# Four edits in the first stage of a fused attention and SwiGLU kernel: a narrower row spread, squares summed in eights, x^T of block 0 copied inside the chip, and one added wait on GpSimd

## The chip, the cores and the metric

The kernel runs on one core of one Trainium2 chip. A core has a matrix engine (TensorE, PE in the profile, with its weight loads listed apart as PEld), a vector engine (VectorE, DVE), an activation engine (ScalarE, ACT), a general engine (GpSimd, POOL) and a queue processor that mostly starts transfers (SyncE, SP). Each engine works through its own instruction list in order and waits on semaphores. SBUF is the core's working memory of 128 partitions; PSUM holds TensorE's results. Transfers (DMAs) are carried by 16 DMA engines, which all queues share.

The metric is the time of one execution on the device in microseconds (us), lower is better.

## The reference

One input x of 2048 tokens by 512 features goes through a layer norm; the result feeds both a 32-head softmax attention (head size 16) and a SwiGLU feed-forward of width 1792, and the two are combined by a gate:

```python
xn = _layernorm(x, axis=-1)
s = _A_ref(xn, A_wqkv, A_wo)                             # attention, 32 heads of 16, then wo
g = _silu(_B_ref(xn, B_w_gate, B_w_up, B_w_down))        # (silu(xn @ w_gate) * (xn @ w_up)) @ w_down
return x + s * g
```

All of it is float32. The kernel keeps the accuracy by splitting every operand of a projection into a high part and a low part (`hi`, `lo`), and multiplying high by high, low by high and high by low.

## The kernel before, in words

The order of all instructions is written out by hand (`tc.manual_schedule()`); what a person orders in the source is the order in which each engine gets its instructions. Waits between engines come from what each instruction reads and writes.

The first stage, which all four edits concern, is the projection of x to queries, keys and values. The 2048 tokens are worked in four blocks (`NB`) of 512 tokens. A block has four token tiles of 128 tokens. Per token tile: `load_tile` brings x in, `stats`, `rates` and `norm` (VectorE) make the layer norm, and `turn_x` transposes it on TensorE (L538), casts the high part on ScalarE (L541) and subtracts to get the low part on VectorE (L544). The transposed x of a block, `xt`, has two sets of buffers that blocks use in turn. With a block's last token tile, GpSimd's queue stores both parts to DRAM (`xt_d`, L547).

Each block then has twelve slots of work, each of 12 matmuls into one PSUM bank from a ring of four (`pps`). Eight are feature tiles (128 features of q or k, `feature_tile`, matmuls at L561): ScalarE casts the bank into `parts` (L600) and squares it into `sq` (L601), VectorE subtracts the low part (L602), and SP stores `parts` to `q_d` or `k_d` (L604). `parts` has three buffers, `sq` five. Four are value tiles (`value_tile`, matmuls at L563), which ScalarE copies out (L615). They store nothing until the block's last one, when the whole block's values go to `v_d`. Block 0 does its value tiles first, the other blocks do them last. While block b is projected, block b + 1 is loaded, normed and transposed between the slots.

The squares are summed by heads with a small bf16 matmul (`squares`, L568), four in one group, since each uses a quarter of a bank's rows. They wait in `pend`, and go out when four are there, or when a block is finished by `flush`. The largest sum bounds the softmax's exponent: in block 3 it becomes one number, `s4`, which two matmuls with a single contraction row spread over partitions and 512 columns (L706 and L707). ScalarE copies the results to `shift` (L708), which four DMAs of GpSimd's queue store, and into rows of the first query tile (L711).

The feed-forward works from `fx`, a copy of x^T laid out so that each half of the partitions (0 to 63 and 64 to 127) holds all 512 features. `load_fx(b, j)` fills it for part j (high, low) of block b with four DMAs of 512 KB on SP's queue, each of which writes 64 partitions; for block 0 this is done in the fifth feature slots of blocks 1 and 2, from `xt_d`. Weights of the feed-forward follow on the same queue.

At the very start, GpSimd makes the low parts of the value weights (`split_w` with GpSimd, L481) while VectorE works on the norm of the first token tiles (L533).

Behind the first stage come 32 units of attention, with feed-forward matmuls (L171) filled in between by a pace that is worked out in the source (`share`), and at the end the output projection.

Of the kernel before, what the change touches and what calls it, by code (L numbers as in the profile page):

```python
# [9 lines left out]
F32 = mybir.dt.float32  # L10
# [15 lines left out]
NB = 4  # L26
# [9 lines left out]
HALF = 64  # L36
# [10 lines left out]
def tile_block(ctx: ExitStack, tc: tile.TileContext, x, wqkv, wo, w_gate, w_up, w_down, out):  # L47
# [93 lines left out]
        dve.tensor_copy(wd[:, f, 0], wdr[i])  # L141
        dve.tensor_sub(wd[:, f, 1], wdr[i], wd[:, f, 0].bitcast(F32))

    def load_fx(b, j):
        for h in range(2):
            dst = fx[h * HALF:(h + 1) * HALF, j].bitcast(F32).rearrange("p (c u) t -> u p c t", u=2)
            for u in range(2):
                sp.dma_start(dst[u], xt_d[b, j, u * HALF:(u + 1) * HALF])


    after = []
# [228 lines left out]
    def finish(u):  # L380
        g, b = divmod(u, NB)
        normalise(u, 0, TB)
        if g % 2:
# [4 lines left out]
            else:  # L388
# [2 lines left out]
                split_o(lhs[b, DT - 1], o2)  # L391
                ready[b] += 1

    units = NG * NB
    steps = KT // 2

# [42 lines left out]
    with ExitStack() as pro:  # L439
        pc = pro.enter_context(tc.tile_pool(name="pc", bufs=1))  # L440
        p2 = pro.enter_context(tc.tile_pool(name="p2", bufs=2))
        p3 = pro.enter_context(tc.tile_pool(name="p3", bufs=3))
        p5 = pro.enter_context(tc.tile_pool(name="p5", bufs=5))
        plast = pro.enter_context(tc.tile_pool(name="plast", bufs=1))
        pps = pro.enter_context(tc.tile_pool(name="pps", bufs=4, space=PSUM))

# [27 lines left out]
        def split_w(m, engine=dve):  # L474
            if m < 8:
                hi, lo = wh[:, m], wl[:, m]
            else:
                hi = vh[:, m - 8].rearrange("p (c f) -> p c f", f=P)
                lo = vl[:, m - 8].rearrange("p (c f) -> p c f", f=P)
            nc.scalar.copy(hi, wraw[m])  # L480
            engine.tensor_sub(lo, wraw[m], hi.bitcast(F32))  # L481

        worder = [8, 9, 10, 11, 0, 1, 2, 3, 4, 5, 6, 7]

# [45 lines left out]

        def norm(t):
            xn[t] = two.tile([P, D], F32, tag="th", name="xn")
            dve.tensor_scalar(xn[t], xin[:, t], mv[:, t, 0:1], rs[:, t:t + 1], op0=ALU.subtract, op1=ALU.mult)  # L533

        def turn_x(b, t, between=None):
            a = acc[t % 2]
            for c in range(DT):
                nc.tensor.transpose(a[:, c * P:(c + 1) * P], xn[t][:, c * P:(c + 1) * P], ident)  # L538
            hi, lo = (xt[b % 2][j][:, :, t * P:(t + 1) * P] for j in range(2))
            av = a.rearrange("p (c f) -> p c f", f=P)  # L540
            nc.scalar.copy(hi, av)  # L541
            if between:
                between()
            dve.tensor_sub(lo, av, hi.bitcast(F32))  # L544
            if t == NT - 1:
                for j in range(2):
                    pool.dma_start(xt_d[b, j], xt[b % 2][j].bitcast(F32))  # L547

# [28 lines left out]

        stats(0)
        rates(0, 1)
        split_w(8, pool)  # L580
        norm(0)
        split_w(9, pool)
        turn_x(0, 0, partial(later, 1))
        for m in (10, 11):
# [48 lines left out]
        for b in range(NB):  # L633
# [3 lines left out]
            for n, (make, i) in enumerate(slots):  # L637
                if b == 0:
                    if n + 5 < 12:
                        load_w(worder[n + 5])  # L640
                    if n >= 2 and n + 2 < 12:
                        split_w(worder[n + 2], pool)
                if n == (1 if b else 2) and more:
                    load_x(b + 1)
                if b in (1, 2) and n == 5:
                    load_fx(0, b - 1)
                if b == 2 and n in (6, 7):
                    load_gu(n - 6)
                if b == 2 and n == 8:
                    load_wd(0)  # L650
                if not more and n == 2:
                    split_gu(0)
                    for bank in acc:
                        dve.memset(bank, 0.0)
                if b == NB - 1 and n == 8:
                    for c in range(2):
                        load_k(0, c)
                    load_q(0)
                    for c in range(2):
                        load_v(0, c)  # L660
                if b == 0 and n == 1:
                    rates(2, NT)
                    norm(2)
                    norm(3)
                made = make(b, i)
                if b == 0 and n == 1:
                    for t in (2, 3):
                        turn_x(0, t)
                if n == 0 and b == 1:
                    flush(0)  # L670
                elif len(pend) == 4:
                    add()
                if make is feature_tile:
                    pend.append(made)
                if b == 0 and n == 11:
                    ring(0, 2, one)
                    queries(0, one)
                if more:
                    if 2 <= n < 6:
                        stats(n - 2)  # L680
                    if n == 5:
                        rates(0, NT)
                    if 6 <= n < 10:
                        norm(n - 6)
                    if 8 <= n < 11:
                        turn_x(b + 1, n - 8)
                    if n == 10:
                        turn_x(b + 1, NT - 1)
                if n == 8 and b:
                    flush(b)  # L690
                if not more and n == 8:
                    dve.reduce_max(pk, peak, axis=AX.X)
                    dve.tensor_add(sm, pk[:, 0:1], pk[:, 1:2])
                if not more and n == 9:
                    tops = pps.tile([P, 512], F32, tag="ps", name="tops")
                    nc.tensor.transpose(tops[0:1, :P], sm, ident)
                    dve.reduce_max(s4, tops[0:1, :P], axis=AX.X)
                    dve.tensor_scalar(s4, s4, 0.51, None, op0=ALU.mult)
                    dve.tensor_scalar(flag, s4, LIMIT, None, op0=ALU.is_le)
                    dve.tensor_scalar(sel[:, :NG * NB], row[:, :NG * NB], s4, None, op0=ALU.mult)  # L700
                    for h in range(2):
                        dve.tensor_copy(selq[:, h * HALF:h * HALF + 1], s4)
                    fill(3 * DC)
                if not more and n == 10:
                    low, high = [pps.tile([P, 512], F32, tag="ps", name="low") for _ in range(2)]
                    mm(high[:2 * NG * NB], sel, row, start=True, stop=True, skip_group_check=True)  # L706
                    mm(low[:HALF + 2], selq, row, start=True, stop=True, skip_group_check=True)  # L707
                    act(shift, high[:2 * NG * NB], AF.Copy, scale=-1.0)  # L708
                    for h in range(2):
                        two_rows = slice(h * HALF, h * HALF + 2)  # L710
                        act(qst[0][two_rows], low[two_rows, None, :].to_broadcast([2, 2, 512]), AF.Copy, scale=-1.0)  # L711
                    for j in range(4):
                        pool.dma_start(sh_d[:, j * 512:(j + 1) * 512], shift.bitcast(F32))

# [54 lines left out]
    prev = None  # L769

    exps = []
    settled = mybir.DependencyInfo(mybir.DependencyClass.Sync, mybir.DependencyReason.DATA)
    for u in range(units):
        g, b = divmod(u, NB)
        q = qst[u % 2]
# [102 lines left out]
```

## Time and profile before

| | us |
|---|---|
| median of 3 runs | 1460.91 |
| lowest and highest | 1458.57, 1462.61 |
| the profiled execution | 1459.36 |
| its span, first to last instruction | 1457.6 |
| granted TensorE clock, mean over the span | 0.998 |

The profile is that of one execution. Its page gives the busy time of each engine, and the chain that ended last: what each piece of work waited for, followed back from the end. Two more kinds of view are used below. A timeline row has the start in us, the duration in us (with several instructions merged, from the first start), engine, line, operation, output and inputs, shape, count, and in brackets how long the engine was idle before and what ended that. A row by windows has the stretch in us, its length, the busy time of each engine, the granted TensorE clock as a share of full speed, the share of the DMA engines' time in use, and the GB/s they moved.

| stretch of the span, us | TensorE busy, us | DMA share | GB/s |
|---|---|---|---|
| 20 to 40 | 20.00 | 0.87 | 304 |
| 40 to 60 | 20.00 | 0.80 | 281 |
| 60 to 80 | 20.00 | 0.99 | 265 |
| 80 to 100 | 20.00 | 0.90 | 326 |
| 100 to 120 | 20.00 | 0.92 | 225 |
| 120 to 140 | 18.27 | 0.94 | 341 |
| 140 to 160 | 20.00 | 0.64 | 173 |

### The profile page before, as it was taken

What the parts mean: (1) busy time and instruction counts of PE and PEld (TensorE: products, weight loads), DVE (VectorE), ACT (ScalarE), POOL (GpSimd) and SP (SyncE); (2) the same over time, 40 slices, a digit from 0 to 9 for tenths busy, and PEclk for the clock granted to TensorE, in tenths of its full rate; (3) what the DMA queues carried; (4) which work ended last, traced back from release to release, by engine and by line L of the source; (5) the groups of instructions that cost most, each with busy time, mean ns of one, the idle gap of its engine ahead of it and who ended that gap; (6) DMA issues with size and microseconds to landing.
All of it is one profiled execution on the core that took longest, in us unless ns stands there. A gap on an engine that the chain in (4) does not pass through costs nothing.

```text
span 1457.6 us, 26766 instructions
## 1 busy us (share of the span) xinstructions
PE 1441.6 (99%) x11237; PEld 806.6 (55%) x11237; DVE 537.7 (37%) x905; ACT 1094.5 (75%) x1219; POOL 88.2 (6%) x105
## 2 busy tenths in 40 slices
PE   9999999999999999999999999999999999999997
PEld 7777655555555555555555555555555555555544
DVE  6543343124333432234233422343243314334535
ACT  4433588788878887888788878887888778887774
POOL 4100200000000000000000000000000000000234
PEclk9999999999999999999999999999999999999999
DMA  8889652033273331143715311437135202423252
GB/s 267 272 284 287 168 121 58 15 86 88 67 172 84 92 78 34 39 110 72 171 36 120 87 24 34 105 86 171 56 76 130 56 12 46 105 63 128 91 188 73
DMA packets 129556, 154.92 MB, mean 106 GB/s; under 512 B 12700, under 2 KB 79260, under 8 KB 128404
## 3 DMA queue, kind: packets, MB, share of 16 engines
q1 hardware_dynamic: 123940, 130.38, 36.0%
q0 software_dynamic: 5200, 22.22, 4.0%
q8 instruction: 91, 1.49, 0.4%
q10 hardware_dynamic: 288, 0.52, 0.1%
q14 instruction: 37, 0.30, 0.1%
HBM read 111.13 MB, written 41.94 MB: 105 GB/s over the span
## 4 chain that ended last, share of the span: by engine, by line
PE 95%; ACT 2%; DVE 1%; DMA 1%; issue 0%; DVEq 0%; ACTq 0%
PE acc L364 32%; PE bankx L171 29%; PE score L785 20%; PE ps L561 6%; PE banky L171 4%; PE ps L563 3%; ACT pr L787 1%; DMA q_d<-parts 1%; PE acc L538 0%; DVE facc L354 0%; PE bankx L326 0%; DMA facc<-in_A_x_dram 0%; DVE y L835 0%; DVE xn L533 0%; DVE y L838 0%
## 5 line engine op out<-in xcount | busy, mean ns | idle before, releaser
L787 ACT ACTIVATE pr<-score 128x1024 f32<-128x1024 f32 x1024 | 992.5, 1023 | 237.7 <-PE score L785 235.0
L364 PE MATMUL acc<-pr,vst 128*17 128x512 f32 x4096 | 489.2, 595 | 0.0
L785 PE MATMUL score<-qst,kst 50*128 50x512 f32 x2048 | 360.1, 424 | 2.9 <-ACT pr L787 2.0
L785 PEld LDWEIGHTS score<-qst,kst 50*128 50x128 f32 x2048 | 177.8, 184 | 273.2 <-ACT pr L787 236.7
L171 PE MATMUL bankx<-fx,guh 64*128 64x512 f32 x896 | 288.4, 392 | 0.0
L171 PE MATMUL banky<-fx,guh 64*128 64x512 f32 x896 | 288.3, 391 | 0.0
L364 PEld LDWEIGHTS acc<-pr,vst 128*17 128x17 f32 x4096 | 93.9, 96 | 235.4 <-issue 234.6
L199 DVE SCALAR_TENSOR_TENSOR ga<-th,bankx 128x512 f32<-128x512 f32 x56 | 38.5, 687 | 464.1 <-ACT th L198 464.1
L171 PEld LDWEIGHTS bankx<-fx,guh 64*128 64x128 f32 x896 | 165.8, 185 | 32.7 <-issue 0.4
L171 PE MATMUL bankx<-fx,gul 64*128 64x512 f32 x448 | 175.4, 391 | 0.0
L171 PE MATMUL banky<-fx,gul 64*128 64x512 f32 x448 | 175.3, 391 | 0.0
L171 PEld LDWEIGHTS banky<-fx,guh 64*128 64x128 f32 x896 | 165.7, 185 | 4.1
L171 PE MATMUL bankx<-wd,hh 64*128 64x512 f32 x672 | 165.8, 389 | 0.0
L171 PE MATMUL banky<-wd,hh 64*128 64x512 f32 x672 | 165.7, 388 | 0.0
L171 PEld LDWEIGHTS bankx<-wd,hh 64*128 64x128 f32 x672 | 124.0, 184 | 24.9
L171 PEld LDWEIGHTS banky<-wd,hh 64*128 64x128 f32 x672 | 124.0, 184 | 2.1
L171 PEld LDWEIGHTS bankx<-fx,gul 64*128 64x128 f32 x448 | 82.8, 185 | 17.5
L171 PEld LDWEIGHTS banky<-fx,gul 64*128 64x128 f32 x448 | 82.8, 185 | 1.8
L561 PE MATMUL ps<-xt,wh 128*128 128x512 f32 x256 | 80.9, 397 | 0.0
L131 DVE TENSOR_TENSOR gul<-gur,guh 128x1024 fp32r<-128x1024 f32 x56 | 68.6, 1226 | 2.1
L218 DVE COPY facc<-bankx 128x512 f32<-128x512 f32 x16 | 11.1, 691 | 131.1 <-PE banky L171 103.9
L600 ACT CAST parts<-ps 128x512 fp32r<-128x512 f32 x32 | 18.7, 585 | 52.0 <-PE ps L561 24.4
(146 smaller groups left out, 1042.7 us busy)
## 6 DMA issues: line engine op xcount, KB each, us to landing
fx<-xt_d SPq DMA_DIRECT2D x32, 512.0 KB
gur<-in_B_w_gate_dram SPq DMA_DIRECT2D x56, 256.0 KB
gur<-in_B_w_up_dram SPq DMA_DIRECT2D x56, 256.0 KB
wdr<-in_B_w_down_dram SPq DMA_DIRECT2D x56, 256.0 KB
kst<-k_d SPq DMA_DIRECT2D x192, 64.0 KB
qst<-q_d SPq DMA_DIRECT2D x192, 64.0 KB
xt_d<-xt POOLq DMA_DIRECT2D x8, 1024.0 KB, 8.0
q_d<-parts SPq DMA_DIRECT2D x16, 512.0 KB
```

Of the source, the lines that this page charges most:

```text
L131: dve.tensor_sub(lo, raw, hi.bitcast(F32))
L171: mm(bank, lhs[h], rhs[h], start=start, stop=stop)
L199: dve.scalar_tensor_tensor(ga, th, 1.0, bankx, op0=ALU.add, op1=ALU.mult)
L218: dve.tensor_copy(facc[:, t], bankx)
L364: mm(a[h * 32:h * 32 + DH + 1], v[:, kt % CT, h * (DH + 1):(h + 1) * (DH + 1)], probs[2 * i + h // 2][:, h % 2], start=kt == 0, stop=kt == ...
L561: mm(ps, w, a[:, c], start=n == 0, stop=n == 3 * DT - 1)
L563: mm(ps, a[:, c, tokens], w, start=n == 0, stop=n == 3 * DT - 1)
L600: nc.scalar.copy(parts[:, 0], ps)
L785: mm(score[j][:, h], k[r, j, kc * P:(kc + 1) * P], q[r, j], start=True, stop=True)
L787: exps.append(act(pr, score[j], AF.Exp, scale=0.25))
```

## The change

Four edits.

- The row spread multiplies only 8 columns of the row of ones, and ScalarE reads column 0 of the result broadcast to 512.
- The group of four squares within a block is gone. All eight of a block go out together, at the first slot of block 1 for block 0 and behind the first value tile for the others. `sq` gets nine buffers.
- Block 0's `xt` is no longer stored to `xt_d`. `load_fx` for block 0 reads `xt` in SBUF instead of DRAM, and is called in block 0's slots 8 and 10 (before the fifth and the seventh feature tile) instead of in blocks 1 and 2.
- GpSimd's first subtraction (`split_w(8, pool)`) gets a wait for VectorE's norm of tile 0.

```diff
-    def load_fx(b, j):
+    def load_fx(b, j, src=None):
+        src = xt_d[b, j] if src is None else src.bitcast(F32)
         for h in range(2):
             dst = fx[h * HALF:(h + 1) * HALF, j].bitcast(F32).rearrange("p (c u) t -> u p c t", u=2)
             for u in range(2):
-                sp.dma_start(dst[u], xt_d[b, j, u * HALF:(u + 1) * HALF])
+                sp.dma_start(dst[u], src[u * HALF:(u + 1) * HALF])
...
-        p5 = pro.enter_context(tc.tile_pool(name="p5", bufs=5))
+        p5 = pro.enter_context(tc.tile_pool(name="p5", bufs=9))
...
-            engine.tensor_sub(lo, wraw[m], hi.bitcast(F32))
+            return engine.tensor_sub(lo, wraw[m], hi.bitcast(F32))
...
-            dve.tensor_scalar(xn[t], xin[:, t], mv[:, t, 0:1], rs[:, t:t + 1], op0=ALU.subtract, op1=ALU.mult)
+            return dve.tensor_scalar(xn[t], xin[:, t], mv[:, t, 0:1], rs[:, t:t + 1], op0=ALU.subtract, op1=ALU.mult)
...
-            if t == NT - 1:
+            if t == NT - 1 and b:
                 for j in range(2):
                     pool.dma_start(xt_d[b, j], xt[b % 2][j].bitcast(F32))
...
-        split_w(8, pool)
-        norm(0)
+        part = split_w(8, pool)
+        tc.add_manual_dep(part.ins, norm(0).ins.name, settled, reason="GpSimd would hold VectorE up")
...
-                if b in (1, 2) and n == 5:
-                    load_fx(0, b - 1)
+                if b == 0 and n in (8, 10):
+                    load_fx(0, n // 2 - 4, xt[0][n // 2 - 4])
...
-                elif len(pend) == 4:
-                    add()
...
-                    mm(high[:2 * NG * NB], sel, row, start=True, stop=True, skip_group_check=True)
-                    mm(low[:HALF + 2], selq, row, start=True, stop=True, skip_group_check=True)
-                    act(shift, high[:2 * NG * NB], AF.Copy, scale=-1.0)
+                    mm(high[:2 * NG * NB, :8], sel, row[:, :8], start=True, stop=True, skip_group_check=True)
+                    mm(low[:HALF + 2, :8], selq, row[:, :8], start=True, stop=True, skip_group_check=True)
+                    act(shift, high[:2 * NG * NB, 0:1].to_broadcast([2 * NG * NB, 512]), AF.Copy, scale=-1.0)
                     for h in range(2):
                         two_rows = slice(h * HALF, h * HALF + 2)
-                        act(qst[0][two_rows], low[two_rows, None, :].to_broadcast([2, 2, 512]), AF.Copy, scale=-1.0)
+                        act(qst[0][two_rows], low[two_rows, None, 0:1].to_broadcast([2, 2, 512]), AF.Copy, scale=-1.0)
```

More of the change, by code (lines that the diff above doesn't have):

```diff
@@ L392, in finish @@
                 ready[b] += 1
+    settled = mybir.DependencyInfo(mybir.DependencyClass.Sync, mybir.DependencyReason.DATA)
     units = NG * NB
@@ L771, in tile_block @@
     exps = []
-    settled = mybir.DependencyInfo(mybir.DependencyClass.Sync, mybir.DependencyReason.DATA)
     for u in range(units):
```

## The prediction

> **What bounds the kernel now.** I read the page first. TensorE is busy for 99% of the span and carries 95% of the chain that ended last, so the time is TensorE's work plus the holes in it. The profiled execution took 1459.36 us around a span of 1457.6.
>
> ```profile
> span 1457.6 us, 26766 instructions
> PE 1441.6 (99%) x11237; PEld 806.6 (55%) x11237; DVE 537.7 (37%) x905; ACT 1094.5 (75%) x1219; POOL 88.2 (6%) x105
> PE 95%; ACT 2%; DVE 1%; DMA 1%; issue 0%; DVEq 0%; ACTq 0%
> ```
>
> All four edits lie in the first 168 us (projections, blocks 0 to 3). The work behind that starts when the last projection tile is copied, and is TensorE-bound, so what the front gains or loses arrives at the end one to one. Second view: the chain in order of time, for the front's last part (start, us, what).
>
> ```profile
> 124.77 0.70 DVE parts L602
> 125.48 10.05 DMA q_d<-parts
> 136.77 0.38 PE bankx L568
> 145.73 2.80 PE ps L563 x12
> 160.73 1.00 PE low L706 x2
> 161.73 1.00 PE low L707 x2
> 162.73 4.56 PE ps L563 x12
> 167.31 0.59 ACT vt L615
> ```
>
> A tile (12 matmuls) takes 2.80 us. Three losses stand out: a wait for a q_d store before the squares at 136.77, 2.00 us for the shift row (L706, L707), and a tile of 4.56 us behind it. I write F0 to F7 for a block's feature tiles (they store to q_d, k_d) and V0 to V3 for its value tiles (they don't).
>
> **The change part by part.**
>
> **1. GpSimd behind tile 0's norm.** Third view, the timeline by engine:
>
> ```profile
> 5.38 1.27 POOL L481 TENSOR_TENSOR vl<-wraw,vh 128x512 fp32r<-128x512 f32 x1 [4.06 <-ACT vh L480]
> 5.77 1.16 DVE L533 TENSOR_SCALAR xn<-facc,mv,rs 128x512 f32<-128x512 f32 x1
> 42.63 0.54 DVE L533 TENSOR_SCALAR xn<-facc,mv,rs 128x512 f32<-128x512 f32 x1
> 8.86 2.53 POOL L481 TENSOR_TENSOR vl<-wraw,vh 128x512 fp32r<-128x512 f32 x2 [0.73 <-ACT vh L480]
> 10.38 1.29 DVE L533 TENSOR_SCALAR xn<-facc,mv,rs 128x512 f32<-128x512 f32 x1
> ```
>
> The norm takes 0.54 alone and 1.16 beside GpSimd's subtraction: 0.62 to win. But GpSimd's four subtractions then run back to back from about 6.4 to 11.5, and the norm of tile 1 (asked for near 9.8) either slips in between two of them (ends near 10.6, gain up to 0.95 after the value tile's wait) or waits for the last (11.8 against 11.67, loss 0.15). Behind the new wait on GpSimd stand only those subtractions, which V0's late matmuls need near 11.5. I take +0.5; step 3 makes it worthless.
>
> **2. Squares in eights.**
>
> ```profile
> 61.86 0.40 PE L561 MATMUL ps<-xt,wl 128*128 128x512 f32 x1
> 62.19 0.40 PE L568 MATMUL bankx<-sq,ind 128*32 128x512 bf16 x4
> 62.52 0.74 PE L561 MATMUL ps<-xt,wh 128*128 128x512 f32 x2
> 136.77 0.38 PE L568 MATMUL bankx<-sq,ind 128*32 128x512 bf16 x1 [1.73 <-ACT sq L601]
> 135.64 0.58 ACT L600 CAST parts<-ps 128x512 fp32r<-128x512 f32 x1 [5.32 <-DMA q_d<-parts]
> ```
>
> Matmuls start every 0.233 us (2.80 / 12). Without the group the next would start at 62.09; it starts at 62.52, and the pair takes 0.74 where 0.63 is usual: a group of four costs 0.54. The second four of eight add 0.23 to 0.33, so each of the four merges saves 0.21 to 0.31, about 0.25. The hole of 1.73 before 136.77 exists because the square of F3 is wanted one tile after F3; with no squares there TensorE goes on into free banks: -1.7. The nine buffers cost nothing (eight wait, one is written). The new demand: at block 1's first slot the group needs the square of F7, made one tile before.
>
> **3. Block 0's copy.** Removed: two 1 MB stores of x^T near 18 us and their two issues on GpSimd's queue (1.39 us behind 6.64 idle, so nothing waits for them), and 2.1 MB loads in blocks 1 and 2. Added: the same two loads, each 4 issues of 512 KB, from SBUF, on SP's queue in block 0, ahead of the stores of F4 and of F6. Their price is the rate. The view by windows (us; busy of PE, PEld, DVE, ACT, POOL; PEclk, DMA share, GB/s), the DMA sizes, and SP's, GpSimd's, ScalarE's and VectorE's rows:
>
> ```profile
> 36.00:38.50 2.50, 2.50 (x16) 1.67 (x16) 1.83 (x3) 1.29 (x4) 1.29 (x1) 1.00 1.03 364
> 49.00:52.50 3.50, 3.50 (x18) 2.45 (x17) 1.39 (x3) 1.09 (x2) 2.82 (x3) 1.00 0.98 398
> 69.00:76.00 7.00, 7.00 (x36) 5.33 (x35) 4.71 (x15) 2.91 (x6) 0.00 (x0) 1.00 1.07 206
> 78.00:81.00 3.00, 3.00 (x16) 2.42 (x16) 1.24 (x2) 0.85 (x3) 0.00 (x0) 1.00 1.05 390
> fx<-xt_d SPq DMA_DIRECT2D x32, 512.0 KB
> 35.00 1.63 SPq L604 DMA_DIRECT2D q_d<-parts  x2
> 65.16 2.70 SPq L148 DMA_DIRECT2D fx<-xt_d  x4
> 67.96 5.48 SPq L604 DMA_DIRECT2D k_d<-parts  x3
> xt_d<-xt POOLq DMA_DIRECT2D x8, 1024.0 KB, 8.0
> 18.03 1.39 POOL L547 DMA_DIRECT2D xt_d<-xt  x2 [6.64 <-ACT xt L541]
> 46.49 0.57 POOL L547 DMA_DIRECT2D xt_d<-xt  x1 [5.82 <-ACT xt L541]
> 47.85 0.59 ACT L600 CAST parts<-ps 128x512 fp32r<-128x512 f32 x1 [1.66 <-issue]
> 53.92 0.58 ACT L600 CAST parts<-ps 128x512 fp32r<-128x512 f32 x1 [2.19 <-PE ps L561]
> 55.04 0.69 DVE L602 TENSOR_TENSOR parts<-ps,parts 128x512 fp32r<-128x512 f32 x1 [1.39 <-ACT sq L601]
> ```
>
> A block's load (issued at 65.16) fills all DMA engines at 206 GB/s: 2.1 MB take 10.2 us. The three stores issued behind it from 67.96 move at 390 GB/s only from about 78: the queue serves in order. In block 1 that was hidden, because after F7 come four value tiles that store nothing. In block 0 the next tiles are block 1's features, and `parts` has three buffers: a tile's cast waits until the store three tiles back has landed.
>
> What sets the rate? Both load and copy write 64 partitions per DMA; the stores at 364 to 390 read 128. So the copy takes no less than 10.2 if writing limits it, and up to 20.4 if reading the same 64 partitions shares what limits; 5.4 (at 390) if HBM was the limit. I take 10.2, the row of the same destination. The Trainium skill ("SBUF — State Buffer", Door 1) says partitions 0 to 63 reach half of the 16 DMA ports, some 218 GB/s, which the 206 fits; "DMA: Bandwidth & Descriptors" (Where 436 GB/s comes from) lets SBUF-to-SBUF run to 435 GB/s, which would make it 4.8 us and speak for the first rival.
>
> The queue after the change: the stores issued at 35.00 end near 38.8, first copy to 49.0, F4's store (0.52 MB, 1.35 us) 50.3, F5's 51.7, second copy 61.9, F6's 63.2; and GpSimd's 2.1 MB (46.49, at 398 GB/s in 49 to 52.5) take 5.3 us of the same engines: F6 lands near 68.7. The cast of block 1's F1 needs that buffer: 68.7 instead of 53.92. Its bank comes free 1.8 us later (53.92 to 55.73), at 70.5 with 0.2 for the release, and F5, which uses that bank, started at 62.52: **+8.2 us**, whatever was won earlier, so step 1 and the first merge count nothing. (Part of it shows earlier, at the eight squares: F7's cast, 47.85 before, waits for F4's store, 50.3 to 55.6.)
>
> Knock-on: block 1's x loads queue behind the same traffic, and VectorE runs their statistics and norms in order with the late subtractions, so the transposes at block 1's eighth slot come 0 to 2 us late; I take 1.9, since the norms are queued directly behind F5's and F6's subtractions. Later on the DMA engines are relieved by two loads of 10.2 us, so I see no stall in blocks 2 and 3.
>
> **4. Shift row.** L706 and L707 take 2.00 us for 512 columns. With 8 columns no row shows the price: 0 at least, at most a group of four 128-column transposes (0.59 below); I take 0.45, saving 1.55. Behind it the clock fell:
>
> ```profile
> 37.48 0.59 PE acc L538 x4
> 162.00:163.00 1.00, 1.00 (x4) 0.30 (x3) 0.00 (x0) 0.59 (x2) 0.35 (x1) 1.00 1.19 247
> 164.00:165.00 1.00, 1.00 (x4) 0.80 (x3) 0.00 (x0) 0.82 (x1) 0.74 (x2) 0.50 0.81 177
> 166.00:167.00 1.00, 1.00 (x4) 0.61 (x2) 0.00 (x0) 0.00 (x0) 0.00 (x0) 0.52 0.32 115
> 162.76 2.05 ACT L711 ACTIVATE qst<-low 2x1024 fp32r<-2x1024 f32 x2 [0.41 <-PE low L707]
> ```
>
> After two microseconds with one row of the array in use the granted clock is 0.50 until 167: the tile takes 4.56 instead of 2.80, 1.76 lost. With the gap a quarter as long I take all of it back (bounds 0 and 1.76): -1.75. ScalarE's broadcast copies (0.59 + 2.05) still fit beside the 2.8 us tile.
>
> The same rule works against the change: the wait of step 3 idles TensorE for several us at a time, so the tiles after it may run at half clock for up to 3.5 us: 0 to +1.75. The hole of 1.73 at 136.77 was followed by no drop. I take +0.9. The Trainium skill ("TensorE: Matmul & The Clock Gate", Part 1) halves the clock after an idle window of about 3.4 us; by it the term would be the full 1.75 and the sum 0.85 higher.
>
> **Sum:** +8.2 + 1.9 + 0.9 - 0.75 (three merges) - 1.7 - 1.55 - 1.75 = **+5.25 us**, 1464.6 against the profiled 1459.36. That execution is 1.55 below the median of 1460.91, on which it gives **1466.2**.
>
> **The rivals.** *Hidden copy, faster.* The copy runs at 390 GB/s, 5.4 us each: F6 lands at 59.1, the bank is free at 60.9, before F5 wants it. Then all gains stand: 0.5 + 1.0 + 1.7 + 1.55 + 1.75 = 6.5, giving 1454.4. For it: the stores' 390. Against: each row at 206. It decides from about 7.6 us per copy (5.25 / 2 less than 10.2). *Slower copy.* Reading and writing the same 64 partitions share: two of the four issues double, 15.3 per copy, +10.2, 1476.4; all four, 1486. Against: no row shows reads and writes disturbing each other. *The clock gain fails* (the gap falls in the same place of a window): 1468. *Step 1 does nothing:* no effect on the forecast.
>
> **How the numbers follow.** A measurement here tells 0.3% (4.4 us) from no change. Forecast and its clock variant 0.62, own range 1461 to 1471; hidden copy 0.23; slower copy 0.15. Slower by over 0.3% (above 1465.3): 0.46 of the first and all of the last, 0.61. Faster (below 1456.5): 0.18 of the hidden copy. Rest 0.21. The range reaches from 1454 to 1479.
>
> **What would show it.** Right: `fx` written between 38 and 65 us at some 200 GB/s; ScalarE's casts in block 1 waiting on q_d and k_d stores; TensorE waiting for squares near 51 us or banks near 62 to 71; no hole near 135; L706 and L707 under 0.5 us, PEclk 1.0 behind. Wrong: GB/s near 390 in that window with casts on time.

## The result and the profile after

| | before | after |
|---|---|---|
| median, us | 1460.10 | 1470.22 |
| lowest and highest, us | 1458.57, 1462.61 | 1469.19, 1471.87 |
| the profiled execution, us | 1459.36 | 1471.00 |
| its span, us | 1457.6 | 1469.2 |
| granted TensorE clock, mean | 0.998 | 0.991 |

The ratio of after to before is 1.0068, 95% interval 1.0056 to 1.0080: some 10 us slower. (The median of before is that of the executions timed beside the changed kernel; with them it moved from 1460.91 to 1460.10.) The forecast was 1466.2.

The page of the changed kernel, its head and the summary of its chain:

```profile
span 1469.2 us, 26759 instructions
PE 1445.0 (98%) x11237; PEld 813.2 (55%) x11237; DVE 536.9 (37%) x905; ACT 1094.2 (74%) x1219; POOL 87.2 (6%) x103
PE 85%; ACT 1%; DVE 1%; issue 0%; DVEq 0%
```

TensorE does the same 11237 matmuls and is busy 3.4 us longer (1441.6 before), and the span grew by 11.6 us, so about 8 us are new idle time and the rest is net slower running (the shift row itself became 1.6 us shorter). The timeline shows where. TensorE's rows of the changed kernel with a wait in brackets, and the shift row (start, duration, engine, line, operation, tiles, shapes, count, idle time before and what ended it; L563 are feature tiles, L570 squares, L706 and L707 the shift row, L784 the first scores):

```profile
53.93 0.38 PE L570 MATMUL banky<-sq,ind 128*32 128x512 bf16 x1 [1.89 <-ACT sq L603]
73.20 1.22 PE L563 MATMUL ps<-xt,wh 128*128 128x512 f32 x2 [6.01 <-DVE parts L604]
171.22 0.28 PE L706 MATMUL low<-row,sel 1*64 1x8 f32 x2
171.42 0.28 PE L707 MATMUL low<-row,selq 1*66 1x8 f32 x2
177.87 1.42 PE L784 MATMUL score<-qst,kst 50*128 50x512 f32 x4 [3.17 <-PEq L717]
```

Three waits: for a square, for a bank, and, behind the shift row, for TensorE's own sequencer at L717, the branch on the flag. The first two come from ScalarE, whose casts are late. Its timeline, the casts of F7 of block 0 and F0 to F2 of block 1:

```profile
52.79 0.59 ACT L602 CAST parts<-ps 128x512 fp32r<-128x512 f32 x1 [5.66 <-DMA k_d<-parts]
60.42 0.59 ACT L602 CAST parts<-ps 128x512 fp32r<-128x512 f32 x1 [6.55 <-DMA k_d<-parts]
71.34 0.59 ACT L602 CAST parts<-ps 128x512 fp32r<-128x512 f32 x1 [9.83 <-DMA k_d<-parts]
73.06 0.59 ACT L602 CAST parts<-ps 128x512 fp32r<-128x512 f32 x1 [0.64 <-DMA k_d<-parts]
```

Each waits for the store that holds its buffer of `parts`. SP's timeline shows what those stores stand behind; its rows of the copies (L149) and the stores (L606):

```profile
38.11 6.16 SPq L149 DMA_DIRECT2D fx<-xt  x4
44.38 4.05 SPq L606 DMA_DIRECT2D k_d<-parts  x2
48.48 5.23 SPq L149 DMA_DIRECT2D fx<-xt  x4
53.80 5.60 SPq L606 DMA_DIRECT2D k_d<-parts  x2
```

And by windows (us; busy of PE, PEld, DVE, ACT, POOL; PEclk, DMA share, GB/s):

```profile
54.00:58.00 4.00, 4.00 (x11) 2.96 (x11) 0.60 (x1) 0.00 (x0) 0.00 (x0) 0.57 1.01 413
60.00:62.00 2.00, 2.00 (x11) 1.61 (x10) 0.46 (x1) 1.08 (x2) 0.00 (x0) 1.00 1.06 200
62.00:68.00 6.00, 5.20 (x23) 3.89 (x21) 1.43 (x3) 0.00 (x0) 0.00 (x0) 1.00 1.06 208
68.00:70.00 2.00, 0.00 (x0) 0.00 (x0) 0.00 (x0) 0.00 (x0) 0.00 (x0) 1.00 1.06 373
72.00:76.00 4.00, 2.80 (x7) 2.22 (x8) 2.48 (x5) 2.59 (x5) 0.00 (x0) 0.50 1.02 388
178.00:181.00 3.00, 3.00 (x15) 3.00 (x17) 0.00 (x0) 1.94 (x2) 0.00 (x0) 0.50 0.87 300
```

The DMA engines are full (share above 1.0) at 200 to 208 GB/s while the second copy runs; from 68 the stores behind it move at 373; F1's cast follows at 71.34, and the bank that F5 wants is free at 73.2. After each of the three waits TensorE runs at a clock of 0.50 to 0.57 in these windows. There is one more such stretch, at the start: behind a wait of 1.46 us for the first transposed x (at 8.73) the trace's records of the clock have 0.50 from 9.97 to 13.39; before has none there.

A ledger by tiles: the start of a tile's first matmul (first score and end of the span in the last rows), after less before; the last column names what came in since the row above (times are cut off at 0.01 us, differences are of the full records):

| tile | before | after | difference | what came in |
|---|---|---|---|---|
| block 0, F4 | 34.17 | 35.61 | +1.43 | start-up: x and the second weight part came later, +0.41 at V0; then half clock from 10 to 13 |
| block 1, F0 | 47.60 | 48.53 | +0.93 | first merge of squares, -0.5 |
| block 1, F1 | 50.83 | 54.23 | +3.40 | the eight squares wait 1.89, and the group |
| block 1, F2 | 53.72 | 58.67 | +4.95 | half clock from 54 to 58 |
| block 1, F5 | 62.51 | 73.20 | +10.69 | bank wait 6.01, less the group that stood here |
| block 1, F6 | 65.41 | 78.38 | +12.98 | half clock from 72 on |
| block 1, V1 | 74.63 | 87.81 | +13.18 | second four of eight, no wait at the transposes |
| block 3, F4 | 131.77 | 144.69 | +12.92 | a merge in block 2 |
| block 3, F5 | 137.07 | 147.49 | +10.42 | no hole, no group of squares |
| block 3, V3 | 162.65 | 171.63 | +8.97 | shift row shorter by 1.6 |
| first score | 168.15 | 177.87 | +9.72 | gap at the branch |
| end | 1457.55 | 1469.20 | +11.65 | half clock behind the gap |

### The profile page after: what moved, and what is told of

Its sections match the earlier page's. It is cut to its first block, busy times and chain, and to the rows that moved or that the text cites. A ratio compares the mean times of both kernels' runs of the same rounds, so it can differ in the third digit from the quotient of the medians.

```text
span 1469.2 us, 26759 instructions
## 1 busy us (share of the span) xinstructions
PE 1445.0 (98%) x11237; PEld 813.2 (55%) x11237; DVE 536.9 (37%) x905; ACT 1094.2 (74%) x1219; POOL 87.2 (6%) x103
## 4 chain that ended last, share of the span: by engine, by line
PE 85%; ACT 1%; DVE 1%; issue 0%; DVEq 0%
PE acc L365 32%; PE bankx L172 30%; PE score L784 20%; PE banky L172 4%; ACT pr L786 1%; DVE facc L355 0%; PE bankx L327 0%; DVE y L834 0%; DVE y L837 0%; DVE y L337 0%; DVE y L338 0%; PE score L843 0%; DVE fx L239 0%; DVE y L177 0%; DVEq L873 0%
## 5 line engine op out<-in xcount | busy, mean ns | idle before, releaser
L784 PE MATMUL score<-qst,kst 50*128 50x512 f32 x2048 | 360.7, 425 | 4.8 <-PEq L717 3.2
L784 PEld LDWEIGHTS score<-qst,kst 50*128 50x128 f32 x2048 | 178.6, 185 | 274.2 <-ACT pr L786 233.0
L563 PE MATMUL ps<-xt,wh 128*128 128x512 f32 x256 | 83.8, 409 | 6.0 <-DVE parts L604 6.0
L563 PEld LDWEIGHTS ps<-xt,wh 128*128 128x128 f32 x256 | 49.6, 196 | 20.7 <-DVE parts L604 6.4
```

Of the source, the lines that this page charges most:

```text
L563: mm(ps, w, a[:, c], start=n == 0, stop=n == 3 * DT - 1)
L784: mm(score[j][:, h], k[r, j, kc * P:(kc + 1) * P], q[r, j], start=True, stop=True)
```

## The experiments

All ratios are to the kernel before, on the same chip, with 95% intervals; "changed" is the changed kernel.

| kernel | median, us | ratio | interval |
|---|---|---|---|
| changed | 1470.22 | 1.0068 | 1.0056 to 1.0080 |
| the copy alone | 1471.57 | 1.0076 | 1.0063 to 1.0090 |
| changed without the copy | 1455.34 | 0.9969 | 0.9959 to 0.9979 |
| the shift row alone | 1461.67 | 1.0009 | 1.0000 to 1.0018 |
| squares in eights alone | 1456.68 | 0.9976 | 0.9966 to 0.9987 |
| the wait on GpSimd alone | 1459.39 | 0.9989 | 0.9980 to 0.9998 |
| changed, copies of 128 partitions | 1458.52 | 0.9991 | 0.9982 to 0.9999 |
| changed, copies from DRAM | 1467.78 | 1.0052 | 1.0039 to 1.0065 |
| the copy alone, four buffers of `parts` | 1471.35 | 1.0075 | 1.0062 to 1.0089 |
| changed, copies in slots 3 and 5 | 1469.11 | 1.0062 | 1.0049 to 1.0075 |
| squares in eights and the wait on GpSimd | 1455.26 | 0.9966 | 0.9952 to 0.9979 |
| changed without the copy, row one slot earlier | 1457.55 | 0.9975 | 0.9966 to 0.9984 |
| changed without the copy, no branch | 1452.68 | 0.9946 | 0.9932 to 0.9959 |

### One edit at a time

Undoing and doing parts. First the kernel before with the copy alone:

```diff
-                if b in (1, 2) and n == 5:
-                    load_fx(0, b - 1)
+                if b == 0 and n in (8, 10):
+                    load_fx(0, n // 2 - 4, xt[0][n // 2 - 4])
...
-            if t == NT - 1:
+            if t == NT - 1 and b:
```

> The kernel before with the copy edit alone (block 0's x^T copied from SBUF in block 0's slots 8 and 10, its stores to DRAM gone). Theory A, the copies hold the queue ahead of the stores: the banks' wait at block 1's F5 as in the changed kernel, first score some 10 to 13 us later than before, the whole 9 to 13 us slower (1469 to 1473). Here the squares come in fours, so the wait for squares in block 1 may fall at F4 instead. Rival B, the squares in eights make the wait (they want the square of F7 one tile after it): this kernel within 3 us of before.

Measured: 1.0076, 11.1 us more (0.0076 of 1460). The copy alone costs all that the change lost. Its waits on TensorE stand in the same places (squares here go in fours, so that the long one is at the group after F4, L569):

```profile
53.71 0.38 PE L569 MATMUL banky<-sq,ind 128*32 128x512 bf16 x1 [1.60 <-ACT sq L602]
71.96 0.59 PE L569 MATMUL bankx<-sq,ind 128*32 128x512 bf16 x1 [6.20 <-ACT sq L602]
```

Then the changed kernel with those lines taken back:

> The changed kernel with the copy edit undone; norm wait, squares in eights and the narrow shift row stay. Theory A: no wait in block 1, no hole in block 3; squares save about 1.2 us in four merges and 2 us in block 3's hole, the shift row 0.8 us at the first score (the branch behind it is the floor): 3 to 5 us faster than before, 1455 to 1457. If the shift row gave all that I predicted (3.3 us), 1453 to 1454. Rival B: still slower than before by several us, with a wait at block 1's first slot.

Measured: 1455.34, ratio 0.9969: the other three edits together win some 4.5 us. This is faster than both kernels.

The shift row alone (the part of the diff at L706 to L711):

> The kernel before with the narrow shift row alone. Theory C, the conditional branch of TensorE (L717, 5.2 us in both traces, started as L706 starts) is the floor of the first score: the last value tile starts 1.6 us earlier and runs at full clock, but the first score only 0.5 to 1.0 us earlier, with a TensorE gap of about 3 us ahead of it and half clock behind it: -1 to +1.5 us on the whole. My prediction's reading (the 3.3 us arrive in full): 1456.8, 3.3 us faster.

Measured: 1.0009, at best nothing. The prediction's 3.3 us are not there. The squares alone (`bufs=9`, and the two lines `elif len(pend) == 4: add()` out):

> The kernel before with the squares in eights alone. By the ledger of the two traces each merge is worth about 0.3 us and the hole in block 3 about 2 us: 3 us faster, 1457. Rival B: slower, with a wait for squares at block 1's first slot.

Measured: 0.9976, -3.5 us. The wait on GpSimd alone:

> The kernel before with only the wait of GpSimd's first subtraction for the norm of tile 0. Theory (the prediction's step 1: the first value tile may start up to 0.5 us earlier, but with the rest of the kernel as before this reaches the end): 0 to -0.5 us. Rival (the added wait lets GpSimd's four subtractions push the norm of tile 1 and the second weight's low part back, which is where the changed kernel's first value tiles lost 1.4 us): +1 to +2 us. The start of the first value tiles has varied by about 1 us between executions of kernels with the same start, so a difference under 1 us is told by the medians and not by one trace.

Measured: 0.9989, -1.6 us with an interval of -2.9 to -0.3, while its profiled execution ended 0.05 us after that of before. The norm did become quicker, 1.16 to 0.55 us, but what it brings at the end is not settled: the median of before itself moved between 1459.49 and 1461.05 from one set of executions to another, and V1 of block 0 started anywhere from 12.1 to 14.5 us in the profiles of all kernels here. In five of these fourteen profiles (changed, the copy alone, the shift row alone, squares alone, squares and the wait), so with the added wait and without it, TensorE ran at a clock of 0.50 for 3.41 us between 8.6 and 13.4, which costs V1 about 1 us.

### What makes the copy slow

Its source, the place in SBUF that it writes, or its place in the queue? First the copies of the changed kernel as two DMAs of 128 partitions instead of four of 64:

```diff
+        if b == 0:
+            dst = fx[:, j].bitcast(F32).rearrange("p (c u) t -> u p c t", u=2)
+            for u in range(2):
+                sp.dma_start(dst[u], src)
+            return
```

> The changed kernel, but each copy of block 0 goes as two DMAs that write all 128 partitions from all 128, instead of four that write 64 from 64: same bytes, packets, source and place in the queue. The second half of the partitions then holds other data than it should, so the feed-forward of block 0 is not the reference's; the work done is the same. Theory A with the rate set by the half of the partitions: 370 to 400 GB/s while it copies, F6's store lands near 60, no or little wait for banks at block 1's F5, 1455 to 1459, near the kernel without the copy (1455.3). Rival D, the rate comes from SBUF-to-SBUF copying or from the packets: 200 GB/s stays, 1468 to 1472.

Measured: 1458.52, 11.7 us less than the changed kernel, with the same bytes in the same slots. The windows in which the copies run, and TensorE's two waits, both in block 1:

```profile
38.00:45.00 7.00, 7.00 (x38) 5.84 (x37) 3.71 (x7) 4.22 (x9) 1.29 (x1) 1.00 1.03 378
45.00:50.00 5.00, 5.00 (x22) 3.77 (x21) 2.37 (x4) 1.81 (x4) 3.48 (x5) 1.00 1.03 371
62.92 0.73 PE L568 MATMUL ps<-xt,wh 128*128 128x512 f32 x2 [0.89 <-DVE parts L609]
75.79 0.66 PE L545 MATMUL acc<-ident,xn 128*128 128x128 f32 x4 [1.41 <-DVE xn L540]
```

371 to 378 GB/s instead of about 206; the bank wait falls from 6.01 to 0.89. The transposes at block 1's eighth slot now wait 1.41 for the norms: this is the prediction's knock-on, which the changed kernel does not show, because there TensorE itself is 11 us late and the norms are done in time.

Then the same slots and destination, with DRAM as the source:

```diff
-            if t == NT - 1 and b:
+            if t == NT - 1:
...
-                    load_fx(0, n // 2 - 4, xt[0][n // 2 - 4])
+                    load_fx(0, n // 2 - 4)
```

> The changed kernel with block 0's x^T stored to DRAM as before and loaded from there, in the same slots 8 and 10 of block 0. Theory A, place and destination make the loss: about 205 GB/s, the same wait at block 1's F5, 1468 to 1473. Rival D, the source in SBUF makes it: 1455 to 1460.

Measured: 1467.78, still 1.0052. In the second copy's windows, and the same two waits:

```profile
60.00:62.00 2.00, 2.00 (x10) 1.64 (x9) 1.64 (x3) 0.00 (x0) 0.00 (x0) 1.00 1.06 211
62.00:66.00 4.00, 2.73 (x12) 1.88 (x10) 0.00 (x0) 0.00 (x0) 0.00 (x0) 1.00 1.06 211
53.02 0.38 PE L570 MATMUL banky<-sq,ind 128*32 128x512 bf16 x1 [2.37 <-ACT sq L603]
71.79 1.22 PE L563 MATMUL ps<-xt,wh 128*128 128x512 f32 x2 [7.06 <-DVE parts L604]
```

211 GB/s from DRAM and 200 to 208 from SBUF: the source does not matter, and the 64 partitions do. Since the wide copy changes how many partitions are read as well as written, and the DRAM one leaves only the writing, writing 64 partitions is enough to set this rate; whether reading 64 would do the same by itself was not run. The Trainium skill ("SBUF — State Buffer", Door 1) gives partitions 0 to 63 half of the ports, some 218 GB/s, and the rows agree. The 435 GB/s that the Trainium skill names for SBUF to SBUF ("DMA: Bandwidth & Descriptors", Where 436 GB/s comes from) is worked out there from all 16 ports; 371 to 378 were seen here over all 128 partitions.

### Can the queue be eased

A fourth buffer of `parts`, with the copy alone:

```diff
-        p3 = pro.enter_context(tc.tile_pool(name="p3", bufs=3))
+        p3 = pro.enter_context(tc.tile_pool(name="p3", bufs=4))
```

> The kernel before with the copy alone and a ring of four parts buffers instead of three. Theory A, the coupling is that a cast waits for the store of as many tiles back as there are buffers: F6's late store then holds block 1's F2 instead of F1, so the bank wait moves from F5 to F6 and is one tile (2.8 us) shorter: 2.3 to 3.3 us less than the copy alone (1471.6), 1468 to 1469.5. Rival: the casts wait for something else in the queue, no change, 1471 to 1473.

Measured: 1471.35, nothing won. The early wait (1.60) is gone, but the long one stays; TensorE and ScalarE:

```profile
71.14 0.59 PE L569 MATMUL bankx<-sq,ind 128*32 128x512 bf16 x1 [8.31 <-ACT sq L602]
70.01 0.59 ACT L601 CAST parts<-ps 128x512 fp32r<-128x512 f32 x1 [9.94 <-DMA k_d<-parts]
```

With four buffers it is F2's cast, not F1's, that waits for the store of F6, and with squares in fours the group after F4 wants F2's square. The store lands at the same time, near 70, and TensorE finds another way to wait for it.

The copies earlier, in slots 3 and 5 (before V3 and before F1) instead of 8 and 10 (before F4 and before F6):

```diff
-                if b == 0 and n in (8, 10):
-                    load_fx(0, n // 2 - 4, xt[0][n // 2 - 4])
+                if b == 0 and n in (3, 5):
+                    load_fx(0, n // 2 - 1, xt[0][n // 2 - 1])
```

> The changed kernel with the same two copies issued in block 0's slots 3 and 5 (ahead of the last value tile and of the second feature tile) instead of 8 and 10. Theory A, it is the place in the queue: the copies run near 22 to 42 us, where block 0's stores to DRAM are gone, F2 and F3 land a little late and the four banks cover it, no wait in block 1: 1454 to 1458. Rival D, copying in SBUF costs wherever it stands: 1465 and more.

Measured: 1469.11, a miss by 11 us or more. Block 1 has no wait, as expected, but block 0 has; ScalarE, GpSimd and TensorE:

```profile
49.89 0.59 ACT L602 CAST parts<-ps 128x512 fp32r<-128x512 f32 x1 [11.03 <-DMA q_d<-parts]
52.05 1.27 POOL L483 TENSOR_TENSOR wl<-wraw,wh 128x512 fp32r<-128x512 f32 x1 [11.82 <-ACT wh L482]
52.81 1.11 PE L540 MATMUL acc<-ident,xn 128*128 128x128 f32 x4 [9.94 <-DVE xt L546]
```

A cast of block 0 now waits 11.03 us for a q_d store behind the second copy, and behind that cast on ScalarE stand the last weight's high part and the transposed x of block 1. With a store every 2.8 us and three buffers, neither place that was tried in block 0's queue has room for copies of 10 us.

### What the shift row runs beside

> The kernel before with squares in eights and the wait on GpSimd, without the shift row's edit and without the copy: what stands against the changed kernel without the copy (1455.3) is the shift row alone. Theory (TensorE's branch of over 5 us behind the shift row sets the first score, so shortening the row gives nothing, and the idle time it leaves costs a little by the half clock): 1454.5 to 1456, no slower than with the shift edit. Rival (the prediction's part 4, the row's 1.55 and the clock's 1.75 are won): 1458 to 1459, some 3 us slower than with it.

This is the kernel before with the squares and the wait on GpSimd, and the changed kernel without the copy differs from it by the shift row alone. Measured: 1455.26 against 1455.34. Shortening the row is worth nothing, as expected. (This pair shows the row alone: in the profile of this kernel V3 ran at full clock behind the wide row, 3.07 us from its first start to its last end, against 4.62 in before. The shift row alone, further up, had both the row and the clock to win, and won neither.) The first scores of the two (this one first; the shift row of the other at 157.50):

```profile
158.19 1.07 PE L705 MATMUL low<-row,sel 1*64 1x512 f32 x2
165.10 0.93 PE L783 MATMUL score<-qst,kst 50*128 50x512 f32 x4 [1.84 <-SPq L716]
```

```profile
157.50 0.28 PE L705 MATMUL low<-row,sel 1*64 1x8 f32 x2
164.07 1.25 PE L783 MATMUL score<-qst,kst 50*128 50x512 f32 x4 [3.09 <-PEq L716]
```

From the row's start to the first score it is 6.91 us with 512 columns and 6.57 with 8. The views leave branches out, but the trace has their records on TensorE (start and duration, us):

```
              load of the flag   branch          first score
before        160.68             161.28  5.20    168.16
changed       171.24             171.84  5.14    177.87
without copy  157.51             158.11  5.06    164.07
squares, wait 158.21             158.90  5.35    165.10
row earlier   155.68             156.28  6.50    164.15
```

TensorE's sequencer reads the flag as the shift row starts, and is then in the branch for over 5 us, while the matmuls handed over before (the row and V3's twelve) run. What is shortened among them leaves TensorE idle longer, except for what reaches past the branch: in before V3 ended at 167.28, 0.80 behind the branch's end at 166.48. To see whether the load can be brought forward, the row went ahead of V2 (the block of lines at L704 to L713 moved up to stand before `made = make(b, i)`):

> The changed kernel without the copy, and with the two matmuls of the shift row, and what reads them, one slot earlier: ahead of the value tile V2 instead of behind it. In all kernels so far TensorE's load of the flag starts 0.02 us after the shift row's first matmul, the branch behind it takes 5.1 to 5.7 us, and the first score follows. Theory 1 (TensorE's sequencer is held at the shift row's first matmul until that may start, and from there runs ahead): the load of the flag moves with the row, by about one tile (3 us), the branch is over before V3 has ended, the gap of 3 us behind V3 goes, and the time is 3 to 5 us below that of the changed kernel without the copy, near 1451. Theory 2 (the sequencer runs ahead by a fixed number of matmuls, 14 here: the two of the row and the twelve of V3): the load stays 14 matmuls ahead of the end of V3, the first score comes about 6.1 us after V3's start as before, and the time is within 1 us of 1455.3.

Measured: 1457.55, ratio 0.9975 against 0.9969 with the row in its place: 2.2 us slower by the medians, 0.9 by the ratios, with intervals that overlap. So the 3 to 5 us of theory 1 are not there, and the time alone does not rule theory 2 out. The trace does: the load came 1.38 us before V3's first matmul (157.06) instead of 0.40 (157.92), more than theory 2 allows and far less than theory 1 asked for. The branch took 6.50, to 162.78, and another engine was then last:

```profile
164.15 1.82 PE L783 MATMUL score<-qst,kst 50*128 50x512 f32 x4 [4.12 <-SPq L716]
```

SP branches too. In this kernel it read the flag at 157.02, behind its own DMA issues and later than TensorE, and the idle time of 4.12 us was ended by SP. TensorE's clock was 0.50 from 163 to 170. What sets how far ahead TensorE's load runs stays open. That the branch itself is the price was tried by leaving it out, with the general path behind it:

```diff
-        fast = nc.values_load(flag, min_val=0, max_val=1)
-        with tc.If(fast < 1):
-            with tc.tile_pool(name="gen", bufs=1) as gen:
...
```

> The changed kernel without the copy and without the branch on the flag: the load of the flag and the general path behind it (L716 to L747 of the changed kernel) are left out, so this kernel only holds for inputs whose bound is small enough, as the ones used are. Theory (the branch sets the first score; the matmuls ahead of it run in its shadow): the gap of about 3 us between V3 and the first score goes, and the half clock behind it; first score about 3 us after V3's start instead of 6.15, time 3 to 4.5 us under the 1455.3 of the changed kernel without the copy, near 1451. Rival (with the branch gone the first score waits for something else that was late as well, such as the copies of the shift row on ScalarE or the loads of the first keys and queries): within 1 us of 1455.3.

Measured: 1452.68, ratio 0.9946 against 0.9969, so 2.7 us by the medians and 3.4 by the ratios, just short of what was expected by the one and within it by the other. What was left out is the load of the flag, the branch and the long path that it jumps over, so which of the three takes the time is not told apart. The gap and the half clock behind it are gone; the first score, and the windows from 162 on of this kernel, then of the one with the branch:

```profile
161.88 0.93 PE L750 MATMUL score<-qst,kst 50*128 50x512 f32 x4 [0.72 <-issue]
162.00:164.00 2.00, 2.00 (x16) 1.61 (x16) 0.00 (x0) 1.34 (x2) 0.00 (x0) 1.00 0.88 257
164.00:166.00 2.00, 1.59 (x14) 1.17 (x14) 0.00 (x0) 2.00 (x3) 0.00 (x0) 1.00 1.05 367
```

```profile
162.00:164.00 2.00, 0.00 (x0) 0.00 (x0) 0.00 (x0) 0.00 (x0) 0.00 (x0) 1.00 0.43 121
164.00:166.00 2.00, 1.93 (x10) 1.75 (x12) 0.00 (x0) 1.02 (x2) 0.00 (x0) 0.62 1.00 353
```

So of the two best kernels that keep the general path, the changed one without the copy and the one with only the squares and the wait on GpSimd are equal, at 0.3% under the kernel before.

## Why the prediction was right, and where it was not

The sign, the place and the mechanism of the loss were right, and 1470.2 lies in the range and in the forecast's own range of 1461 to 1471. But against the sum of +5.25 the medians show +10.1 and the profiled executions +11.6, about twice as much. That the time still lies in the own range, 0.8 us under its upper end, is in part luck: a term that was counted twice, the knock-on, made up for some of what the clock and the shift row were wrong by. Point by point:

**The copy's rate** was right: 10.2 us per copy at 206 GB/s was taken, from the row of a load with the same destination; 200 to 211 were measured, and the two experiments on source and partitions show that the reason given, writing 64 partitions, is enough for it. The hidden copy (390 GB/s) is what the wide copies show: 1458.5, where 1454.4 was worked out for a copy that costs nothing.

**The term +8.2 for F5** was right in its path (F6's store, F1's cast, the bank, F5) and came out as 10.69 at F5's start. Where the prediction has F1's cast at 68.7, it stands at 71.34. The step that was mis-sized is the queue's timetable: it was drawn on the times of before, and the profiled execution started its tiles 1.43 later; F7's cast, put at 50.3 to 55.6, came at 52.79 and held the eight squares for 1.89, as the bracket said. GpSimd's 2.1 MB, which the sum puts behind the second copy, moved ahead of it: by the packets in the trace they had some 320 of the 410 GB/s from 52 to 58, and F5's store, put at 51.7, released F0's cast only at 60.42. This changes the order and not the sum. Some 1.4 of the 2.64 us by which F1's cast came later than foretold go back to the start-up; the rest was not taken apart.

**The clock after the waits** was the term furthest off: +0.9 was taken of 0 to 1.75. The ledger has +1.55 behind the wait of 1.89, +2.29 behind the one of 6.01, 1.93 behind the branch's gap, and about 1.0 at the start. The hole of 1.73 in block 3 of before, from which the prediction argued for less, did not lower the clock; the wait of 1.89 did. The records of the clock in the traces tell the two apart. In each of the fourteen profiles all changes of the clock lie whole multiples of 3.41 us from each other (in the changed kernel 54.35, 57.76, 71.41, 78.24, 177.23 and so on), and where these stretches lie differs from one execution to the next. The wait of 1.89, from 52.04 to 53.93, lies inside one stretch, 50.94 to 54.35, and the next stretch is slow; the hole of 1.73 is cut in two by a border at 136.25. So which waits are paid for is in part chance, and in the changed kernel a drop lasted one or two such stretches. The full 1.75, which the prediction put down to the Trainium skill ("TensorE: Matmul & The Clock Gate", Part 1), was nearer to the price of each.

**The knock-on of 1.9** does not exist in the changed kernel (V0 to V1 of block 1 takes 3.86, 3.64 before, and the difference is the second four of squares). It was added to the term above although both come from the same lateness: once TensorE waits for F6's store, VectorE's norms have that time too. Alone, with wide copies, it is real, 1.41.

**The squares**, -0.75 and -1.7: -2.45 for three merges and the hole, some -2.7 with the fourth. Alone they measure -3.5 (-5.0 to -1.9), so the size was about right. But the hole's part does not come on top of the copy. In the kernel with the copy alone, squares still in fours, block 3 has no hole either:

```profile
147.56 0.59 ACT L601 CAST parts<-ps 128x512 fp32r<-128x512 f32 x1 [1.66 <-PE ps L562]
150.24 0.40 PE L569 MATMUL bankx<-sq,ind 128*32 128x512 bf16 x4
```

No cast there waits for a store. That the `fx` loads of 2.1 MB are gone from blocks 1 and 2 would explain it, but this was not tested. It is one reason why the parts don't add up: the copy's +11.1 and the -4.5 of the rest make 6.6, while together they are +9.9. A second is that the early wait was followed by half clock with the squares in eights (1.89 us, +1.55) and not with fours (1.60). The intervals leave about 3 us of room on the difference of 3.3, so it can't be shared out further.

**The shift row and the clock behind it**, -1.55 and -1.75, is the step that failed. The prediction read the chain, which puts the time on TensorE's matmuls one after the other, and took the row of 2.00 and the tile of 4.56 as lost time. The row did become 0.3 to 0.5 us long, and the clock behind it stayed at 1.00, as foretold. But already in before these matmuls ran, all but the last 0.80 us, in the shadow of the branch, which no view counts as busy. From the row's start to the first score it was 7.49 us before and is 6.66 now, so 0.8 us were won at most, and the longer gap was followed by half clock, +1.93, more than that. Nor was the clock's 1.75 a fixed price of the wide row. Where the row's 2.07 us lie inside one of the stretches of 3.41 us (before, the copy alone, the wait on GpSimd alone), V3 ran at half clock; where a border cuts them (squares alone, squares and the wait, four buffers), V3 ran at full clock with the same 512 columns. The case "the clock gain fails" was named, at 1468; that the row's own 1.55 goes with it was not thought of. With both terms at nothing the sum would be +8.55, or 1469.5 on the median.

**Step 1** does no harm, and whether it does more stays open, as told above; in the changed kernel it is swallowed by the wait at F5, as the prediction has it.

## What to carry to other kernels

A transfer's price is its rate times what stands behind it in its queue: look for the buffer ring whose release it delays, count the tiles until that ring comes round, and count the stall only once, since everything that it makes late gets the same time back. Before shortening work ahead of a branch or a join, find when the sequencer gets past it; work that runs in that shadow is free. A loss of clock that one profile shows may not be there in the next execution, so don't book its return as a fixed gain. And test edits alone and by leaving one out: here one of four edits cost 11 us and hid the 4.5 that the others won.

## What the runs showed of the hardware

- TensorE was in its branch for 5.06 to 6.50 us in every kernel that has it, against 0.05 to 0.07 for the branch records of the other engines; SP's next instruction came 3.44 us after its own (162.07 to 165.51 in the profile of before). The matmuls handed over before it keep running.
- A DMA onto 64 partitions ran at 200 to 211 GB/s with all 16 engines full, whether from SBUF or DRAM; one onto 128 at 371 to 378.
- TensorE's granted clock changes only at borders that lie 3.41 us apart, in all fourteen profiles, and where they lie differs between executions. In the changed kernel the waits of 1.89, 6.01 and 3.17 us were followed by 0.50 for 3.41, 6.83 and 6.83 us. After the 1.73 in the kernel before and the 2.37 with the copies from DRAM (53.02, clock 1.00 to 68) it did not fall: a border cuts both, the second at 51.33, so that at most 1.2 and 1.7 us lie in one stretch. The 1.60 with the copy alone lies in one stretch and cost nothing either. How much of a stretch must be idle is not settled by these.
- The Trainium skill ("TensorE: Matmul & The Clock Gate", Part 1) halves the clock after an idle window of about 3.4 us; here waits of 1.84 (squares and the wait, ahead of the first score) and 1.89 us were enough.
- The start of the stage differs between executions by up to 2.4 us at V1 of block 0, about 1 us of it by half clock in the start-up, so a part of any difference between two single traces belongs to neither kernel.
